# Weights on the ScalarE ring beside DMA transposes on the SyncE ring, with a new instruction order, in a mixer-and-MLP block

## The chip, the cores and the metric

The kernel runs on one core of one Trainium2 chip. The metric is device time in microseconds (us), the median of several executions. A profile's span is some 1 to 2.5 us shorter than the time of a whole execution, so spans are compared with spans and times with times. The granted TensorE clock is given as a share of full speed.

The engines: TensorE (PE in the profile, PEld its weight loads), VectorE (DVE), ScalarE (ACT), GpSimd (POOL) and SyncE (SP). SyncE and ScalarE can both issue DMA transfers. Each has its own DMA queue, called its ring here. In the DMA view q1 is the SyncE ring and q10 the ScalarE ring. A transfer's time "to landing" runs from its issue to the signal that it is complete. PSUM is the memory that TensorE's results go to and from which other engines copy them.

## The reference, cut to what matters

```python
B, S, D, F = 1, 2048, 512, 1792            # all bf16
h  = gelu(layernorm(x) @ w1)               # first layer
hs = shift(h, by channel quarter: +1, -1, +2, -2 tokens) @ w2
x1 = x + hs                                # the "mixing" product
return x1 + gelu(layernorm(x1) @ w3) @ w4  # second layer, "up" and "down"
```

Both normalized inputs have to be transposed (tokens to columns) before their product. There are 16 tiles of 128 tokens in each layer, so 32 transposes of 128x512.

## The kernel before

The program is a list of operations with their reads and writes. A small scheduling model, inside the kernel file, orders DVE, ScalarE, GpSimd and SyncE. TensorE's order is given by a script, and the loads' order by another. In the script `up1:g` and `up2:g` are the first and second layer's products over a group of tiles (the tables `GROUPS`), `mix:t` a mixing product and `down:t` a last product. `ty:n` turns tile n on TensorE (n from 16 up is the second layer), `sa` and `sb` turn the halves of tile 0. `warm` is products of zeros, `ra` and `rb` are the halves of tile 0's first-layer product, and `th:0` turns its result; every tile that the script does not name is turned by a DMA transpose on SyncE.

```python
GROUPS = {1: (1, 1, 1, 1, 2, 1, 4, 2, 2, 1), 2: (2, 4, 4, 2, 4)}
LOADS = """
x1 x2 tp2 x0@act w1a w1b x3 x4-5 tp5 w2a w2b x6-7 w3 tp17 w4a x8-10 w4b tp6 x11-12 tp1 tp16 x13-15
"""
SCRIPT = """
warm:9 sa:0 sb:0 ty:1 ra:0 rb:0 ty:2 up1:1 th:0 up1:2 mix:0 ty:3 ty:5 mix:1 ty:4 up1:3-4 ty:16 mix:2 ty:17
mix:3 up2:0 mix:4 up1:5 down:1 down:0 ...
"""
...
            if q not in pe_tp:                      # not named in the script
                pg.add("sp", f"tp{q}",
                       lambda e: e.dma_start(xT[:, :, P * t : P * (t + 1)], xn_buf[:, slot(q), :], transpose=True), ...)
```

So the loads all leave on SyncE except x0 (`@act`), in one ring, and each engine runs its own list strictly in order. The eight tiles that TensorE needs first (0 to 5, and the second layer's 0 and 1) are turned on TensorE itself.

## Time and profile before

| | before |
|---|---|
| time, median (first session) | 135.79 us |
| span | 134.6 us |
| TensorE busy | 130.9 us (97%) |
| DMA transposes / tiles turned on TensorE | 24 / 8 |
| issue to landing of a DMA transpose, median | 2.5 us |
| waits of TensorE | 0.7 us for w1, 0.4 us for the zeros of the warm-up |

The lines that carry this stand in the prediction below. The table says that TensorE is the bound, that it hardly ever waits, and that its first real product waits for w1.

### The profile page before, as it was taken

The numbers are of one execution on the slowest core, as the hardware profiler recorded it, in microseconds if no ns is written. First come the engines' busy times: TensorE is split into PE (matmuls) and PEld (weight loads), VectorE is DVE, ScalarE is ACT, GpSimd is POOL, SyncE is SP. The second block draws the span as 40 slices with busy tenths as digits, with TensorE's granted clock in tenths as the row PEclk, the third lists the DMA queues.
The fourth block names the chain that finished last, engine by engine and source line by source line (L and its number), as shares of the span: only waits on it lengthen the run. The fifth ranks groups of instructions, "written<-read, shape, count | busy, mean of one in ns | idle before, by whom it ended". The sixth has DMA issues, their size and how long they took to land.

```text
span 134.6 us, 2001 instructions
## 1 busy us (share of the span) xinstructions
PE 130.9 (97%) x776; PEld 71.5 (53%) x789; DVE 50.8 (38%) x134; ACT 58.4 (43%) x92; POOL 29.7 (22%) x68
## 2 busy tenths in 40 slices
PE   8799999999999999999999999999999999999994
PEld 3287688544656444478544444444444444444464
DVE  2689996856178930070061004232222200012222
ACT  5779349989544275547315554000000155520000
POOL 2444549892102860006010001200000000000000
DMA  5999998445452134100411000211111100001112
GB/s 136 323 345 399 361 304 234 90 81 105 90 115 85 24 75 98 39 0 0 83 39 39 0 0 0 65 52 44 39 39 53 64 0 0 0 5 39 39 39 78
DMA packets 21289, 12.19 MB, mean 91 GB/s; under 512 B 13856, under 2 KB 20768, under 8 KB 21280
## 3 DMA queue, kind: packets, MB, share of 16 engines
q1 hardware_dynamic: 20704, 11.80, 32.7%
q10 hardware_dynamic: 576, 0.26, 0.7%
q8 instruction: 6, 0.10, 0.3%
q14 instruction: 3, 0.02, 0.1%
HBM read 6.82 MB, written 2.10 MB: 66 GB/s over the span
## 4 chain that ended last, share of the span: by engine, by line
PE 93%; DMA 4%; SPq 1%; issue 1%; DVE 0%
PE y_ps L626 46%; PE o_ps L695 36%; PE o_ps L666 10%; DMA w_sb<-in_w_dram 4%; PE y_ps L490 1%; SPq L368 1%; PE y_ps L528 0%; SPq L377 0%; DVE o_sb L703 0%; PE o_ps L594 0%; SPq L857 0%
## 5 line engine op out<-in xcount | busy, mean ns | idle before, releaser
L626 PE MATMUL y_ps<-xnT,w_sb 128*128 128x512 bf16 (+2 forms) x421 | 63.4, 308 | 0.2
L626 PEld LDWEIGHTS y_ps<-xnT,w_sb 128*128 128x128 bf16 x424 | 38.3, 98 | 24.8
L641 ACT ACTIVATE h2T<-y_ps 128x1024 bf16<-128x1024 f32 (+1 forms) x29 | 28.6, 993 | 48.8 <-PE y_ps L626 48.6
L695 PE MATMUL o_ps<-w_sb,h2T 128*128 128x512 bf16 (+3 forms) x247 | 48.6, 355 | 0.3
L695 PEld LDWEIGHTS o_ps<-w_sb,h2T 128*128 128x128 bf16 x252 | 23.5, 98 | 24.7
L703 DVE TENSOR_TENSOR o_sb<-o_ps,x_sb 128x512 bf16<-128x512 f32 (+3 forms) x18 | 11.4, 632 | 47.1 <-PE o_ps L695 47.1
L423 POOL TENSOR_TENSOR rstd<-mv,neghalf 128x1 f32<-128x1 f32 x21 | 11.5, 549 | 23.6 <-DVE mv L418 14.8
L416 DVE BATCH_NORM_STATS2 st<-x_sb 128x6 f32<-128x512 bf16 x21 | 14.1, 678 | 3.4 <-DMA x_sb<-in_x_dram 3.2
L666 PE MATMUL o_ps<-w_sb,hT 128*128 128x512 bf16 x59 | 14.9, 379 | 0.3
L423 POOL TENSOR_TENSOR rstd<-vpe,neghalf 128x1 f32<-128x1 f32 x11 | 6.0, 547 | 29.4 <-DVE vpe L412 29.3
L673 DVE SCALAR_TENSOR_TENSOR x_sb<-o_ps,x_sb 128x512 bf16<-128x512 f32 x5 | 3.4, 686 | 19.2 <-PE o_ps L666 19.2
L641 ACT ACTIVATE hT<-y_ps 128x512 bf16<-128x512 f32 (+1 forms) x10 | 8.1, 807 | 5.5 <-PE y_ps L626 5.3
L677 DVE TENSOR_TENSOR x_sb<-o_ps,x_sb 128x512 bf16<-128x512 f32 x11 | 7.6, 687 | 4.4 <-PE o_ps L666 4.1
L666 PEld LDWEIGHTS o_ps<-w_sb,hT 128*128 128x128 bf16 x64 | 6.0, 98 | 5.7
L457 POOL TENSOR_SCALAR xn_buf<-x_sb,rstd,nmr 128x512 bf16<-128x512 bf16 x11 | 8.4, 765 | 0.8 <-DVE nmr L450 0.4
L400 ACT ACTIVATE junk<-x_sb 128x512 bf16<-128x512 bf16 x11 | 6.9, 624 | 2.2 <-DVE x_sb L673 2.2
L454 ACT ACTIVATE xn_buf<-x_sb,nmr,rstd 128x512 bf16<-128x512 bf16 x8 | 6.3, 806 | 0.6 <-POOL nmr L450 0.6
L445 DVE TENSOR_SCALAR xn_buf<-x_sb,mv,rstd 128x512 bf16<-128x512 bf16 x12 | 5.3, 442 | 2.8 <-POOL rstd L423 2.6
L720 PE MATMUL o_ps<-zeros 128*128 128x512 bf16 x9 | 4.0, 631 | 0.4 <-DVE zeros L347 0.4
L395 ACT ACTIVATE junk<-x_sb 128x512 bf16<-128x512 bf16 x6 | 3.7, 624 | 0.8 <-DMA x_sb<-in_x_dram 0.8
L418 DVE BATCH_NORM_AGGREGATE mv<-st 128x2 f32<-128x9 f32 x21 | 3.8, 189 | 0.3
L450 POOL TENSOR_SCALAR nmr<-mv,rstd 128x1 f32<-128x1 f32 x13 | 3.4, 263 | 0.7
(34 smaller groups left out, 28.6 us busy)
## 6 DMA issues: line engine op xcount, KB each, us to landing
out_dram<-o_sb SPq DMA_DIRECT2D x15, 128.0 KB, 1.7
w_sb<-in_w_dram SPq DMA_DIRECT2D x1, 1792.0 KB, 9.7
w_sb<-in_w_dram SPq DMA_DIRECT2D x2, 896.0 KB, 11.5
w_sb<-in_w_dram SPq DMA_DIRECT2D x4, 256.0 KB, 5.2
x_sb<-in_x_dram SPq DMA_DIRECT2D x3, 256.0 KB, 5.1
x_sb<-in_x_dram SPq DMA_DIRECT2D x2, 384.0 KB, 8.9
x_sb<-in_x_dram SPq DMA_DIRECT2D x3, 128.0 KB, 2.6
xnT<-xn_buf SPq DMA_TRANSPOSE x24, 2.5
```

What stands on the lines that cost most here:

```text
L400: (lambda d: (lambda e: e.activation(d, src, ACT_F.Square, accum_out=sums[:, q, 1:2])))(junk[:, b, :]),
L416: pg.add("dve", f"bnst{q}", lambda e: e.bn_stats(st9[:, q, 0:6], src), reads=rs, writes=[(("st", q), 0)], dur=605)
L423: lambda e: e.tensor_tensor(col(rstd), var, neghalf[:], ALU.pow),
L445: lambda e: e.tensor_scalar(dst, src, mv[:, q, 0:1], rstd[:, q : q + 1], ALU.subtract, ALU.mult),
L454: f = lambda e: e.activation(dst, src, ACT_F.Identity, bias=nmr[:, q : q + 1], scale=rstd[:, q : q + 1])
L457: f = lambda e: e.tensor_scalar(dst, src, rstd[:, q : q + 1], nmr[:, q : q + 1], ALU.mult, ALU.add)
L626: ins = e.matmul(y_ps[:, p, W * i : W * (i + 1)], wsb[:, dc, P * fc : P * (fc + 1)], src[:, dc, P * t0 : P * t0 + W], start=(dc == 0), sto ...
L641: (lambda d, s: (lambda e: e.activation(d, s, ACT_F.Gelu_apprx_tanh)))(dst, ysrc),
L666: ins = e.matmul(dst, hT[:, j, c0 : c0 + P], w2_sb[:, j, :], start=(j == 0), stop=(j == DC - 1))
L677: f = lambda e: e.tensor_tensor(x1_sb[:, t, :], dst, x_sb[:, t, :], ALU.add)
L695: ins = e.matmul(dst, h2T[:, fc, P * t : P * (t + 1)], w4_sb[:, fc, cs], start=(fc == 0), stop=(fc == FC - 1))
L703: (lambda d, c: (lambda e: e.tensor_tensor(o_sb[:, oi, c], d, x1_sb[:, t, c], ALU.add)))(dst, cs),
```

## The change

The intent is to free TensorE from three transposes and to keep the remaining DMA transposes out of the queue of the big weight loads. w3 and w4, and three pairs of x tiles, leave on ScalarE's ring. Each is held back until a named ScalarE instruction has been issued (`>ev1act`). The order of everything was searched anew with the scheduling model. The core of the diff, other tables and the script's tail cut:

```diff
+        for a, b in self.gates:
+            assert named[a].eng == named[b].eng, (a, b)
+            order_only.add((named[a].idx, named[b].idx))
 ...
-                at = max(clock + 500.0, op.start + 2450.0, last + 600.0) + self.LAG["tp"]
+                at = max(clock + 500.0, op.start + 2450.0, last[op.eng] + 600.0) + self.LAG["tp"]
 ...
-GROUPS = {1: (1, 1, 1, 1, 2, 1, 4, 2, 2, 1), 2: (2, 4, 4, 2, 4)}
+GROUPS = {1: (1, 1, 1, 1, 1, 1, 1, 2, 2, 1, 4), 2: (1, 1, 4, 2, 4, 4)}
 LOADS = """
-x1 x2 tp2 x0@act w1a w1b x3 x4-5 tp5 w2a w2b x6-7 w3 tp17 w4a x8-10 w4b tp6 x11-12 tp1 tp16 x13-15
+x1-2 w3@act>ev1act x0 tp1 x9-10@act>gelu1_3_0 x14-15@act>norm0_1 x3 x12-13@act>norm0_1 w1a tp3 w1b x5 x4 x6
+w4@act>gelu1_4_0 x11 tp4 tp2 w2a w2b x7-8 tp26
 SCRIPT = """
-warm:9 sa:0 sb:0 ty:1 ra:0 rb:0 ty:2 up1:1 th:0 up1:2 mix:0 ty:3 ty:5 mix:1 ty:4 up1:3-4 ty:16 mix:2 ty:17
-mix:3 up2:0 ...
+warm:13 sa:0 ty:2 sb:0 ty:1 ra:0 rb:0 up1:2 ty:3 th:0 up1:1 up1:3 mix:1 ty:4 mix:0 up1:4 mix:2 up1:5 mix:3
+up1:6 mix:4 up1:9 mix:5 up2:1 up1:7 up2:0 ...
```

The changed line with `last[op.eng]` is a belief about the hardware in the model: a transpose waits for earlier loads of its own ring only.

More of the change, by code (lines that the diff above doesn't have):

```diff
@@ L31 @@
     LOOK = {"dve": 300.0, "act": 300.0}
-    DUE = 164483.0
+    DUE = 2578.37
     BEGIN = {"sp": 30.0, "act": 150.0, "pe": 400.0, "dve": 150.0, "pool": 450.0}
@@ L40, in __init__ @@
         self.lines = []
+        self.gates = []
     def add(self, eng, name, fn, reads=(), writes=(), dur=100.0, queue=None):
@@ L161, in place @@
         fed = {}
-        clock = moved = last = self.total = 0.0
+        clock = moved = self.total = 0.0
+        last = {"sp": 0.0, "act": 0.0}
         out = []
@@ L198, in land @@
         def land(op):
-            nonlocal moved, last
+            nonlocal moved
             if op.queue == "tp":
-                at = max(clock + 500.0, op.start + 2450.0, last + 600.0) + self.LAG["tp"]
+                at = max(clock + 500.0, op.start + 2450.0, last[op.eng] + 600.0) + self.LAG["tp"]
             elif op.name.startswith("out"):
@@ L209, in land @@
             if op.queue != "tp":
-                last = max(last, at)
+                last[op.eng] = max(last[op.eng], at)
             op.landed = at
@@ L258, in place @@
         return out
-GROUPS = {1: (1, 1, 1, 1, 2, 1, 4, 2, 2, 1), 2: (2, 4, 4, 2, 4)}
-NORM = {0: "act", 3: "act", 7: "pool", 8: "act", 9: "pool", 10: "pool", 11: "pool", 12: "pool", 14: "act", 15: "act", 16: "pool", 18: "act", 19: "act", 24: "pool", 25: "act", 26: "pool", 27: "pool", 29: "pool", 30: "pool", 31: "act"}
-EVAC = {0: "both", 1: "both", 2: "both", 4: "both", 8: "both", 9: "dve", 10: "dve", 11: "dve", 12: "dve", 13: "dve", 14: "dve", 16: "dve", 17: "dve", 19: "both", 20: "both", 21: "both", 22: "both", 23: "both", 24: "dve", 25: "both", 27: "both", 29: "both", 30: "both", 31: "both"}
-STAT_ACT = (0, 7, 9, 12, 13, 15, 18, 21, 25, 29, 30)
+GROUPS = {1: (1, 1, 1, 1, 1, 1, 1, 2, 2, 1, 4), 2: (1, 1, 4, 2, 4, 4)}
+NORM = {0: "act", 4: "act", 8: "act", 10: "act", 11: "pool", 13: "act", 14: "act", 15: "pool", 16: "act", 18: "pool", 19: "pool", 20: "pool", 21: "act", 22: "act", 24: "pool", 25: "pool", 30: "act", 31: "pool"}
+EVAC = {0: "dve", 1: "both", 3: "both", 4: "dve", 5: "both", 6: "both", 7: "both", 8: "dve", 9: "dve", 11: "dve", 12: "both", 13: "dve", 15: "dve", 16: "both", 17: "both", 18: "dve", 19: "both", 20: "both", 23: "dve", 24: "both", 25: "both", 27: "dve", 30: "both", 31: "dve"}
+STAT_ACT = (0, 15, 16, 17, 18, 21, 24, 25, 29, 30)
 TAIL = (256, 160, 96)
-NMR = {0: "pool", 1: "pool", 3: "pool", 5: "pool", 6: "pool", 7: "pool", 8: "pool", 9: "pool", 11: "pool", 13: "pool", 14: "pool", 15: "pool", 16: "pool", 17: "pool", 18: "pool", 20: "pool", 21: "pool", 22: "pool", 26: "pool", 27: "pool", 28: "pool", 29: "pool", 31: "pool"}
+NMR = {0: "pool", 1: "pool", 4: "pool", 5: "pool", 6: "pool", 7: "pool", 8: "pool", 9: "pool", 10: "pool", 11: "pool", 13: "pool", 14: "pool", 15: "pool", 17: "pool", 19: "pool", 20: "pool", 21: "pool", 24: "pool", 29: "pool", 30: "pool"}
 NAT = (0,)
@@ L268 @@
 CSPLIT = ()
-HEV = {0: "dve", 4: "dve"}
-BIAS = {}
+HEV = {1: "dve", 3: "dve", 6: "dve"}
+BIAS = {"bnag0": 683.678, "bnag11": -581.289, "bnag3": -802.143, "bnag4": -247.442, "bnst1": 1925.74, "bnst10": -711, "bnst18": -352, "bnst7": -21, "mean11": -569, "mean15": -1694, "nmr17": -616, "nmr6": -709, "norm17": 1723.03, "norm3": 232.064, "ssq21": 621.832, "sum9": 1546, "tp13": -978.761, "tp15": 365.734, "tp21": -782, "x1_10": -3, "x1_9": -111}
 LOADS = """
-x1 x2 tp2 x0@act w1a w1b x3 x4-5 tp5 w2a w2b x6-7 w3 tp17 w4a x8-10 w4b tp6 x11-12 tp1 tp16 x13-15
+x1-2 w3@act>ev1act x0 tp1 x9-10@act>gelu1_3_0 x14-15@act>norm0_1 x3 x12-13@act>norm0_1 w1a tp3 w1b x5 x4 x6
+w4@act>gelu1_4_0 x11 tp4 tp2 w2a w2b x7-8 tp26
 """
 SCRIPT = """
-warm:9 sa:0 sb:0 ty:1 ra:0 rb:0 ty:2 up1:1 th:0 up1:2 mix:0 ty:3 ty:5 mix:1 ty:4 up1:3-4 ty:16 mix:2 ty:17
-mix:3 up2:0 mix:4 up1:5 down:1 down:0 mix:5 up1:6-7 mix:8 mix:6 up1:9 mix:9-10 up1:8 mix:7 mix:11 up2:1
-mix:13 mix:15 up2:3 down:5 mix:12 up2:2 mix:14 down:2 down:4 down:3 down:6-8 down:11 down:9 up2:4 down:10
-down:12-15
+warm:13 sa:0 ty:2 sb:0 ty:1 ra:0 rb:0 up1:2 ty:3 th:0 up1:1 up1:3 mix:1 ty:4 mix:0 up1:4 mix:2 up1:5 mix:3
+up1:6 mix:4 up1:9 mix:5 up2:1 up1:7 up2:0 mix:7 mix:6 up1:8 down:0 mix:8 up1:10 mix:10 mix:9 up2:2 mix:14
+down:1 mix:11 up2:3 mix:13 down:2-3 down:6 mix:15 up2:4 mix:12 down:7 down:4-5 down:8-9 up2:5 down:10
+down:12 down:11 down:14 down:13 down:15
 """
@@ L363, in load @@
             name, _, eng = item.partition("@")
-            eng = eng or "sp"
+            eng = eng.partition(">")[0] or "sp"
             if name[0] == "x":
@@ L744, in bass_standalone__mixer_s_mlp__prompt_kernel @@
                     op.first = i - 100
+                    if ">" in item:
+                        pg.gates.append((item.partition(">")[2], op.name))
                     queues[op.eng].append(op.name)
```

## The prediction

> **What bounds the kernel now.** I read the page's busy line first, then the chain that ended last, then the waits and the start in order of time.
>
> ```profile
> PE 130.9 (97%) x776; PEld 71.5 (53%) x789; DVE 50.8 (38%) x134; ACT 58.4 (43%) x92; POOL 29.7 (22%) x68
> PE 93%; DMA 4%; SPq 1%; issue 1%; DVE 0%
> ```
>
> The reader is to see that TensorE is busy for 130.9 of 134.6 us, and that 93% of the chain that sets the end is TensorE itself. The other engines have room over the whole span. The opening part of the chain, in order of time, and two stretches from its middle:
>
> ```profile
> 0.99 0.43 SPq L377
> 1.47 5.13 DMA w_sb<-in_w_dram
> 6.65 0.61 PE y_ps L528 x2
> ...
> 8.60 0.92 PE y_ps L626 x16
> ...
> 12.02 2.64 PE y_ps L626 x32
> ...
> 24.70 6.04 PE o_ps L695 x28
> ```
>
> One wait stands at the head: the second half of w1, issued at about 1.47 us, releases the second half of the first tile's row product (L528) at 6.65 us. After it the chain has only TensorE entries, and no "issue" entry over 0.05 us. The last product ends at 132.87 us, where the chain passes to the last DVE add. So after 6.65 us there are 126.2 us with hardly a gap. The waits of TensorE confirm this; there are only two:
>
> ```profile
> PE y_ps L528 <- DMA w_sb<-in_w_dram: 0.7, 1, 0.7
> PE o_ps L720 <- DVE zeros L347: 0.4, 1, 0.4
> ```
>
> Only two things can move the time much: the TensorE work that stands after w1, and the moment at which w1 lands. New stalls are the third, and they can only add. The busy table by stretch (TensorE, weight load, DVE, ScalarE, GpSimd, clock, DMA share, GB/s) shows where a stall would come easily:
>
> ```profile
> 7.00:17.00 10.00, 9.90 (x112) 7.61 (x112) 9.37 (x26) 6.94 (x14) 4.54 (x9) 1.00 1.05 368
> 17.00:31.00 14.00, 13.95 (x104) 9.41 (x103) 10.23 (x36) 11.54 (x26) 11.40 (x23) 1.00 0.81 172
> 60.00:90.00 30.00, 29.84 (x158) 15.59 (x160) 5.98 (x16) 12.14 (x14) 4.15 (x8) 1.00 0.13 31
> ```
>
> From 7 to 17 us DVE is 94% busy and the DMA engines are full at 368 GB/s. After 60 us nothing but TensorE is loaded. The change acts in the tight part.
>
> **What the Trainium skill says.** "TensorE: Matmul & The Clock Gate", section "Wait — 56ns, not 53.3ns?", gives a warm matmul as its columns over 2.4 GHz plus about 2.5 ns. The trace agrees: 28 products of 512 columns take 6.04 us (216 ns each), and 16 of 128 columns take 0.92 us at most (57 ns each; 16 x 55.8 = 0.89 us). I count work by it. "DMA: Bandwidth & Descriptors", section "Issuing engines are not separate DMA queues", says that transfers issued from ScalarE and SyncE share the same 16 DMA engines, so a second ring saves issue time only. Its section "Queues, rings and completion order" adds that each DMA engine takes turns between rings packet by packet. Before, the ScalarE ring carries a single tile and the last store, so its trace can't show how two loaded rings share. One side of it shows: in one common ring, the first transpose, issued at 15.96 us amid the weight loads, took 5.9 us to land, and the median one 2.5 us.
>
> ```profile
> DMA to landing us min/median/max: 2.4/2.5/5.9
> ```
>
> **The change part by part.**
>
> TensorE transposes. Before, eight tiles are turned on TensorE (tile 0 in halves, 1, 2, 3, 4, 5 and the second-layer tiles 0 and 1). Two of them stand ahead of the first w1 product, in time that is waiting anyway. Six lie on the path. At four 128-column passes of 55.8 ns each that is 6 x 0.223 = 1.34 us. After, five are turned on TensorE (0, 1, 2, 3, 4); 0, 2 and 1 are now before the w1 product, so two lie on the path: 0.45 us. Saved: 0.89 us. The other three go to DMA transposes on the SyncE ring (24 become 27).
>
> Groups. The first layer's products over groups of one tile cost 16 x 55.8 = 0.893 us, of two tiles 16 x 109.2 = 1.747 us, of four 16 x 215.8 = 3.453 us. Before, beside tile 0: five single, three double, one quadruple, 13.16 us. After: seven single, two double, one quadruple, 13.20 us. Cost: 0.04 us. The second layer has 56 products a group: 3.125, 6.115 and 12.085 us. Before (2,4,4,2,4): 48.49 us. After (1,1,4,2,4,4): 48.62 us. Cost: 0.13 us. The mixing products and the down products are the same, and so is the tail of the last tile.
>
> Sum of work on the path: -0.89 + 0.17 = -0.72 us.
>
> The head. Before, SyncE issues x1, x2, w1a, w1b, with x0 on ScalarE. After, SyncE issues x1-2 (one transfer), x0, x3, w1a, w1b. w1b is the fifth issue and no longer the fourth, at some 0.45 us each (0.87 us for the first two), and one more tile of 131 KB lies ahead of it, which at the 330 to 350 GB/s of this stretch is 0.38 us. These two overlap, so I don't add them: w1b lands about 0.4 us later, near 7.0 us. The 13 warming products (9 before, 9 took 4.02 us) and four transposes, by an estimate from the rows of the start, are through at 6 to 6.7 us: still under w1. So the start costs +0.4 us.
>
> The loads. w3 leaves on ScalarE after tile 1's evacuation (some 6.5 us, from a like step at 5.6 to 6.0 us before), x9-10 and the rest after a GELU near 11 us, w4 after another near 14.5 us. Adding the new order's durations from 7.0 us, the second-layer product that first needs w3 comes at 20 us and the first down product at 31 us. Before, w3 took 9.7 us from issue to landing in full queues; from 6.5 us that is 16 us, in time. w4 (11.5 us a half before) lands by about 26 us, in time. Their going earlier or later is worth nothing in itself: both were hidden.
>
> The ordering elsewhere (which engine normalizes or evacuates a tile, the biases) moves work between engines that are not the bound. No gain to count where TensorE has no gaps.
>
> Sum: -0.72 + 0.4 = -0.3 us if nothing stalls. That would be 135.5 us.
>
> **The rivals.**
>
> First, w2 becomes a wait. Before, 1.83 MB go through the ring up to w2b and the first mixing product starts at 9.57 us, its weights loading at 9.30. After, four single tiles and x11 lie ahead of w2b, 2.10 MB; the extra 0.26 MB at 345 GB/s is 0.76 us, so about 10.1 us, while the new order needs it at about 10.6 us (7.0 + 0.45 + three single groups at 0.89 + two transposes at 0.22 + half a product's start). That is a margin of half a microsecond, and w3's packets come in from about 8 us. They are 3,584 bytes a row against w2's 1,024, so if rings take turns by packet w3 gets the larger share. If so the mixing product waits 0.5 to 3 us, and that early in a dense kernel the wait goes straight to the end. Against it: w3's issue is gated, by 8 us most of w2's bytes have gone out.
>
> Second, the transposes beside w3. The new order's first product with a DMA-transposed tile is the single group 5, at about 14.7 us, where before the first such product came at about 22 us. The tile is loaded and normalized by perhaps 10.5 us (some 2.5 us of statistics, power, scale with DVE full). At 2.5 us it lands at 13 us, in time; at the 5.9 us seen amid loads it lands past 16 us and TensorE stands for 1.5 to 2 us. What speaks for the first is the purpose of the change: the transposes are no longer behind the weights in one ring.
>
> Third, ScalarE blocked by issuing. On SyncE the issues behind a full ring took 3.59 us (x8-10) and 1.83 us (w4b), where an ordinary one takes 0.45. The same on ScalarE, for w4 near 14.5 us with x tiles queued ahead, would hold up the GELUs that the mixing products need. SyncE has nothing else to do; ScalarE has, at 69% to 82% busy in the tight stretches. Cost: 0 to 2 us.
>
> Fourth, the start: with the hole in the DMA rate at 2.7 to 3.3 us before (41 to 184 GB/s) the added tile could be free, which gives back up to 0.4 us.
>
> **Range and chances.** The floor is the path without new stalls and with a free head: 135.79 - 0.72 - 0.35 (all remaining gaps closed) = 134.7 us. A gain of over 2% needs 133.1 us, 1.6 us below that, so it is next to excluded. Without stalls it is 135.1 to 135.5; small stalls of 0.2 us or so are likely, and one of the first three rivals in full gives 136.5 to 138. I put a third on one of them costing more than 0.5 us, and a twelfth on them summing to the 2.7 us that make it slower by 2%. I take 135.5 us, with a range of 134.7 to 137.2.
>
> **What would show it.** TensorE transposes (L490) at 20 instructions in place of 32; the first-layer row product's release at about 7.0 us by w1; TensorE's own waits still only w1 and the zeros. If a wait of the mixing product for w2 appears near 11 us, the first rival is right; if one of an up product for a DMA-transposed tile appears at 15 to 18 us, the second; if ScalarE shows issues of 1 us or more and TensorE waits for GELU results, the third. If w1 is released at 6.6 us the fourth holds. The prediction is wrong if the new waits sum to over 2 us, or if the gain is over 1.1 us, which would mean that gaps I counted as 0.35 us in the dense part were larger.

## The result, and the profile after

The changed kernel took 143.3 us (143.04 to 143.81, four runs) against 135.78 us in the same session. The ratio is 1.0554, 95% interval 1.0491 to 1.0617. Ratios here and below are the mean time of one kernel's fast runs over that of the other's of the same rounds, so not quite the ratio of the medians quoted. All four runs: their spans were 140.8 to 142.5 us and their mean clocks 0.976 to 0.988.

The page of the changed kernel: busy time by engine, then three rows of the 40 slices (3.5 us each), then the chain that ended last:

```profile
PE 133.8 (95%) x853; PEld 73.8 (52%) x853; DVE 51.2 (36%) x139; ACT 56.0 (40%) x82; POOL 27.5 (19%) x64
...
PE   8899079999999999999999999999999999999994
...
PEclk9999856999999999999999999999999999999999
DMA  4999999991565421003102112001211100011112
...
PE 86%; DMA 9%; DVE 1%; POOL 1%; SPq 1%; issue 0%; DVEq 0%
```

TensorE has a hole in the fifth slice (14 to 17.6 us). From that slice on the granted clock is down for three slices. The DMA row stays at 9 through the hole. The share of the chain that is DMA has risen from 4% to 9%. The chain in order of time (start, length, what):

```profile
3.06 4.32 DMA x_sb<-in_x_dram
...
9.94 0.41 DVE xn_buf L452
10.35 0.03 DVE mv L425
10.38 8.15 DMA xnT<-xn_buf
18.53 0.05 issue
18.58 1.89 PE y_ps L633 x16
20.47 1.71 PE o_ps L673 x4
```

Tile 5 is scaled by 10.35 us and its transpose is issued at 10.38. It lands at 18.53, after 8.15 us where the median was 2.5 before. Its product follows at once, and 16 matmuls take 1.89 us where 16 took 0.89 us at full clock. TensorE's own list of waits has one large entry:

```profile
PE y_ps L633 <- DMA xnT<-xn_buf: 4.4, 1, 4.4
```

The stretches of the hole (TensorE, weight load, DVE, ScalarE, GpSimd, clock, DMA share, GB/s):

```profile
15.00:16.00 1.00, 0.00 (x0) 0.00 (x0) 0.94 (x3) 0.00 (x0) 0.77 (x2) 1.00 0.81 134
16.00:17.00 1.00, 0.00 (x0) 0.00 (x0) 0.00 (x0) 0.00 (x0) 0.12 (x1) 0.87 1.09 267
17.00:18.00 1.00, 0.00 (x0) 0.00 (x0) 0.00 (x0) 0.00 (x0) 0.00 (x0) 0.50 1.79 198
18.00:19.00 1.00, 0.42 (x5) 0.43 (x6) 0.00 (x0) 0.00 (x0) 0.00 (x0) 0.50 0.83 159
...
23.00:24.00 1.00, 1.00 (x11) 0.83 (x9) 0.73 (x5) 0.17 (x1) 0.91 (x2) 0.71 0.99 316
```

Between 16.2 and 18.5 us no compute engine does anything at all: every one of them stands at a place of its list that needs, directly or through another engine, what this one transpose releases. The DMA engines are busy but move 134 to 267 GB/s, where in the stretch from 7 to 17 us the kernel before moved 368. The clock falls at 16.75 us and is back at 23.6.

The span's account closes. The work on TensorE's path is 0.72 us less, as counted in the prediction. The hole costs 4.41 us. From 18.58 to 23.6 us TensorE works 5.0 us at half clock, which loses 2.5 us. Together that is +6.2 us, and the spans differ by 140.8 - 134.6 = 6.2 us. Whether the 2.5 us could be had back by itself is another question, which the first experiment asks.

### The profile page after: what moved, and what is told of

Same layout as the page of the kernel before. It is cut to its first block, busy times and chain, and to the rows that moved or that the text cites. A ratio compares the mean times of both kernels' runs of the same rounds, so it can differ in the third digit from the quotient of the medians.

```text
span 140.8 us, 2139 instructions
## 1 busy us (share of the span) xinstructions
PE 133.8 (95%) x853; PEld 73.8 (52%) x853; DVE 51.2 (36%) x139; ACT 56.0 (40%) x82; POOL 27.5 (19%) x64
## 3 DMA queue, kind: packets, MB, share of 16 engines
q10 hardware_dynamic: 3584, 4.59, 11.5%
## 4 chain that ended last, share of the span: by engine, by line
PE 86%; DMA 9%; DVE 1%; POOL 1%; SPq 1%; issue 0%; DVEq 0%
PE y_ps L633 43%; PE o_ps L702 34%; PE o_ps L673 9%; DMA xnT<-xn_buf 6%; DMA x_sb<-in_x_dram 3%; POOL rstd L430 1%; DVE st L423 1%; SPq L375 0%; DVE xn_buf L452 0%; SPq L384 0%; POOL nmr L457 0%; DVE o_sb L710 0%; DVE mv L425 0%; DVEq L830 0%
## 5 line engine op out<-in xcount | busy, mean ns | idle before, releaser
L633 PE MATMUL y_ps<-xnT,w_sb 128*128 128x128 bf16 (+2 forms) x496 | 65.6, 294 | 4.4 <-DMA xnT<-xn_buf 4.4
L633 PEld LDWEIGHTS y_ps<-xnT,w_sb 128*128 128x128 bf16 x496 | 41.1, 101 | 29.6 <-DMA xnT<-xn_buf 4.9
L648 ACT ACTIVATE h2T<-y_ps 128x1024 bf16<-128x1024 f32 (+2 forms) x29 | 28.7, 994 | 43.5 <-PE y_ps L633 43.3
L702 PEld LDWEIGHTS o_ps<-w_sb,h2T 128*128 128x128 bf16 x252 | 23.6, 98 | 24.9
L673 PE MATMUL o_ps<-w_sb,hT 128*128 128x512 bf16 x64 | 17.0, 395 | 0.0
L423 DVE BATCH_NORM_STATS2 st<-x_sb 128x6 f32<-128x512 bf16 x22 | 14.7, 674 | 2.8 <-DMA x_sb<-in_x_dram 2.7
L684 DVE TENSOR_TENSOR x_sb<-o_ps,x_sb 128x512 bf16<-128x512 f32 x8 | 5.5, 686 | 21.6 <-PE o_ps L673 21.5
L680 DVE SCALAR_TENSOR_TENSOR x_sb<-o_ps,x_sb 128x512 bf16<-128x512 f32 x8 | 5.4, 686 | 13.6 <-PE o_ps L673 13.6
L407 ACT ACTIVATE junk<-x_sb 128x512 bf16<-128x512 bf16 x10 | 6.2, 624 | 6.6 <-DVE x_sb L680 6.6
L452 DVE TENSOR_SCALAR xn_buf<-x_sb,mv,rstd 128x512 bf16<-128x512 bf16 x14 | 6.5, 465 | 3.8 <-POOL rstd L430 3.8
L464 POOL TENSOR_SCALAR xn_buf<-x_sb,rstd,nmr 128x512 bf16<-128x512 bf16 x8 | 6.1, 770 | 1.1 <-DVE nmr L457 0.9
L727 PEld LDWEIGHTS o_ps<-zeros 128*128 128x128 bf16 x13 | 1.5, 123 | 2.7 <-issue 1.7
```

Of the source, the lines that this page charges most:

```text
L407: (lambda d: (lambda e: e.activation(d, src, ACT_F.Square, accum_out=sums[:, q, 1:2])))(junk[:, b, :]),
L423: pg.add("dve", f"bnst{q}", lambda e: e.bn_stats(st9[:, q, 0:6], src), reads=rs, writes=[(("st", q), 0)], dur=605)
L452: lambda e: e.tensor_scalar(dst, src, mv[:, q, 0:1], rstd[:, q : q + 1], ALU.subtract, ALU.mult),
L464: f = lambda e: e.tensor_scalar(dst, src, rstd[:, q : q + 1], nmr[:, q : q + 1], ALU.mult, ALU.add)
L633: ins = e.matmul(y_ps[:, p, W * i : W * (i + 1)], wsb[:, dc, P * fc : P * (fc + 1)], src[:, dc, P * t0 : P * t0 + W], start=(dc == 0), sto ...
L648: (lambda d, s: (lambda e: e.activation(d, s, ACT_F.Gelu_apprx_tanh)))(dst, ysrc),
```

## The experiments

Three theories stand for the 8.2 us. **A:** a ring is served transfer by transfer, so the transpose waited for all of w3. **B:** the rings take turns packet by packet, so each small packet of a transpose waits for a row of the loads. **C:** what was issued earlier goes first, whatever its ring. A second question is whether the lateness of these few transposes is the whole loss. Line numbers differ between the kernels by a few lines, since the edits add some.

**1. The hole filled.** 18 products of zeros were put ahead of tile 5's product; the order of everything else is unchanged.

```diff
+    pg.add("pe", "fill", fill, reads=[(("zeros",), 0)], writes=pair_rv(p, v - 0.5), dur=0.0)   # 18 x 128x512
     pg.add("pe", f"up{layer}_{g}_{f0}", f, ...      # only for layer 1, group 5
```

> The changed kernel with 18 products of zeros (3.9 us at full clock) put ahead of the first-layer product of tile 5, where TensorE stood still for 4.4 us; nothing else moves. Theory: 4.4 us of the loss is the wait for the DMA transpose of tile 5, and 2.5 us more is the half clock from 16.75 to 23.6 us that the idle time brought (5.0 us of work at half speed). Then the transpose still lands near 18.5 us, the clock stays at 1.00, and the time is about 143.3 - 2.5 = 140.8 us. Rival: the clock fell for another reason, or the stretch after it waits for other transposes anyway; then the time stays at 143 us.

Measured: 142.17 us, ratio 1.0515 (1.0463 to 1.0567), clock 1.00, span 141.9 us. TensorE in order of time:

```profile
14.22 4.05 PE L642 MATMUL y_ps<-zeros 128*128 128x512 bf16 x18
18.95 1.07 PE L633 MATMUL y_ps<-xnT,w_sb 128*128 128x128 bf16 x16 [0.68 <-DMA xnT<-xn_buf]
19.85 1.03 PE L682 MATMUL o_ps<-w_sb,hT 128*128 128x512 bf16 x4
22.28 1.07 PE L633 MATMUL y_ps<-xnT,w_sb 128*128 128x128 bf16 x16 [1.40 <-DMA xnT<-xn_buf]
```

The clock held, so the idle time had brought it down. But the 2.5 us did not come back in full: the two ratios differ by only 0.5 us' worth, and their intervals overlap. (The execution profiled, 143.33 us, is the longest of the four; the others took 141.96 to 142.31.) TensorE at full clock waits for the next transpose, tile 6, until 22.28 us. The changed kernel's own trace says how much could come back. Its first four transposes landed at 18.53, 20.72, 23.13 and 25.29 us, and the product with the last of them began at 26.41. At full clock it could have begun just after 25.29, so some 1 us of the 2.5 was there to be had (an estimate from these landings). The rest was hidden behind the next transposes, which set the pace, one after another.

**2. w3 in four transfers,** as four row blocks (rows of 3,584 bytes as before) and as four column blocks (rows of 896 bytes); everything else is unchanged.

```diff
-   e.dma_start(w3_sb[:], whole)
+   [e.dma_start(dst[:, c : c + 1, :], whole[:, c : c + 1, :]) for c in range(4)]                                    # row blocks
+   [e.dma_start(dst[:, :, cols * k : cols * (k + 1)], whole[:, :, cols * k : cols * (k + 1)]) for k in range(4)]   # column blocks
```

> The changed kernel with w3 issued as four transfers of 448 KB (one after another at the same place on the ScalarE ring, same 3,584-byte rows, same order of everything else). Theory A, a ring is served transfer by transfer: the transpose of tile 5 goes in between two pieces, its landing falls from 8.2 us to 4 to 5 us, and TensorE's wait from 4.4 to about 1 us, 139 to 140 us. Theory B, the sharing goes by packets and the size of w3's rows is what counts: no change, 8 us and 143 us. Theory C, everything issued earlier goes first whatever its ring: no change either.

> The changed kernel with w3 issued as four column blocks: 448 KB each again, but rows of 896 bytes in place of 3,584. Theory A, transfer by transfer: as with the four row blocks, 4 to 5 us for the transpose of tile 5. Theory B, packet by packet: here too it gets its turns, four times as often, so its landing falls to 4 to 5 us while the row blocks leave it at 8 us. Theory C, order of issue whatever the ring: still 8 us in both.

Measured: 144.01 us (ratio 1.0634, 1.0562 to 1.0705) and 145.06 us (1.0711, 1.0638 to 1.0784). Tile 5's transpose took 8.4 and 8.6 us to land. Theory A falls. Theory B in the form "the size of w3's rows counts" falls as well. The packet records of the trace show why neither edit could help: in the changed kernel the transpose's first packet was moved at 14.25 us, 3.9 us after its issue, just as the last of w3's 512 rows had started (14.24). After that its packets went beside the x tiles that follow on the same ring more than beside w3.

**3. Tiles 5, 6, 11 and 17 back on TensorE,** first right ahead of their use, then one mixing product earlier.

```diff
-up1:5 mix:3 up1:6 mix:4 up1:9 mix:5 up2:1
+ty:5 up1:5 mix:3 ty:6 up1:6 mix:4 ty:11 up1:9 mix:5 ty:17 up2:1                  # e2_pe_tp
-mix:2 up1:5 mix:3 up1:6 mix:4 up1:9 mix:5 up2:1
+ty:5 mix:2 up1:5 ty:6 mix:3 up1:6 ty:11 mix:4 up1:9 ty:17 mix:5 up2:1            # e6_pe_ahead
```

> The changed kernel with tiles 5, 6 and 11 of the first layer and tile 1 of the second turned on TensorE again (4 x 0.22 = 0.9 us more work). Theory: the DMA transposes of these early tiles are the whole loss; the stall of 4.4 us and the half clock (2.5 us) both go, so 143.3 - 6.9 + 0.9 = 137.3 us, down to 136.5 if the time before outside the span shrinks too. Rival: the next DMA-transposed tiles (7, 8, then tile 0 of the second layer) are as late, so that a stall of 1 us or more comes up near 22 to 26 us and the time stays above 139 us.

> The changed kernel with tiles 5, 6, 11 and second-layer tile 1 turned on TensorE, this time one mixing product ahead of their use, so that the evacuation is hidden (with the turn just ahead of its use TensorE waited 0.8 to 0.9 us for the copy four times, 140.7 us). Theory: the loss is the lateness of these four DMA transposes and nothing else; what remains over before is 0.17 us of work: 135.5 to 137 us. Rival: more comes up later (transposes of tiles 7, 8 and second-layer tile 0 while w4 flows): above 138 us.

Measured: 140.71 us (ratio 1.041, 1.0357 to 1.0464) and 139.28 us (1.0279, 1.025 to 1.0309). In the first form TensorE waits 0.8 to 0.9 us four times, because the copy out of PSUM stands right between turn and use; that edit was clumsy. In the second form a single wait is left:

```profile
PE y_ps L633 <- DMA xnT<-xn_buf: 1.9, 1, 1.9
```

So turning these four tiles on TensorE takes away about half of the loss (1.0554 to 1.0279), although it adds some 0.9 us of work. The rival of the expectation was right about the rest. The next DMA transposes, of tiles 7 and 8, are late too: up to 6.9 us to land.

**4. w4 held back** in that second form, until just ahead of the first second-layer GELU.

> The version with tiles 5, 6, 11 and second-layer tile 1 turned on TensorE one product ahead (139.3 us), with w4 alone held back on ScalarE until just ahead of the first second-layer GELU (near 22 us in place of 13.5). Theory: the 1.9 us that TensorE still waited there for the transpose of tile 7 or 8 (6.9 us from issue to landing) is w4's doing; without it those transposes land in 3 us and the wait goes: 137.2 to 138 us, as long as w4 lands before the first down product (near 33 us). Rival: the x tiles on that ring are what delays them, and the wait stays at 1.5 us or more; or w4 becomes the wait, which gives 139 us or more.

Measured: 143.33 us (the three fast runs of four; 143.91 with the slow one), ratio 1.0623 (1.0586 to 1.066). The 137.2 to 138 us of the theory were missed. Its first half came true: the transposes of tiles 7 and 8 landed after 3.0 and 2.5 us, and the wait for them is gone; TensorE runs through from 20.89 to 25.9 us. Then it waits for the transpose of second-layer tile 0, which now lies beside w4:

```profile
PE y_ps L633 <- DMA xnT<-xn_buf: 4.0, 1, 4.0
```

The chain in order of time shows its length:

```profile
21.52 8.31 DMA xnT<-xn_buf
```

The 8.3 us follow the load to wherever it is put.

**5. ScalarE's loads held back** in the changed kernel: w3 and the x tiles until 13.3 us; then only the x tiles and w4.

```diff
+   held = [op for op in pg.seq if op.name in ('dma_w3', 'dma_x9', 'dma_x14', 'dma_x12')]   # to just ahead of dma_w4
+   held = [op for op in pg.seq if op.name in ('dma_x9', 'dma_x14', 'dma_x12', 'dma_w4')]   # to just ahead of gelu1_5_0
```

> The changed kernel with the order of all compute unchanged, but w3 and the three x transfers held on ScalarE until just ahead of w4 (near 13.4 us instead of 6.4 and 10.5 to 11.9 us). Theory: without loads on the other ring the transpose of tile 5 takes about 2.5 us from issue to landing (lands near 13 us), tile 6 lands near 14.2, and TensorE does not wait for either; instead the first product with w3 waits some 3 us near 19 to 22 us. Time 138 to 140.5 us. Rival: the transposes are slow in this stretch for a reason of their own (the busy SyncE ring[...]): landing stays at 6 us or more with the ScalarE ring silent.

> The changed kernel with w3 where it is (6.4 us), but the three x transfers and w4 held until ahead of the GELU of tile 5 (near 14.5 us). Theory: the delay has two parts, a start behind w3 and a slow passage beside the rows that follow it; w3 alone lets the transpose of tile 5 land right after w3's last rows, near 15 to 16 us in place of 18.5, so TensorE waits about 1 to 1.5 us. If only w3 counts, no change to 18.5 us; if only the x rows count, it lands near 13 us.

Measured, w3 held: 143.71 us, ratio 1.0606 (1.0556 to 1.0657). Tile 5's transpose landed after 4.3 us in place of 8.2, and TensorE waited 0.41 us for it. So most of the lateness goes with the other ring's traffic. The expected 2.5 us were not reached: 449 of its 512 packets were moved between 11 and 12 us, the others only by 13.65, and why is not shown. The second half of the expectation failed: w3's rows ran from 14.45 us on, tile 6's transpose landed only at 18.56, after 7.1 us, and TensorE waited 2.15 us for it:

```profile
14.52 1.07 PE L633 MATMUL y_ps<-xnT,w_sb 128*128 128x128 bf16 x16 [0.41 <-DMA xnT<-xn_buf]
...
18.61 1.07 PE L633 MATMUL y_ps<-xnT,w_sb 128*128 128x128 bf16 x16 [2.15 <-DMA xnT<-xn_buf]
```

The transposes that followed were late too, and the time did not move:

```profile
PE y_ps L633 <- DMA xnT<-xn_buf: 6.9, 4, 2.7
```

Measured, x tiles held: two runs of 140.19 and 142.6 us, and the profile counts as slow by that spread, so no time is drawn from them. The trace, of the longer run, gives 6.3 us to landing for tile 5's transpose and a wait of 2.43 us for it. Its landing lies between that of the changed kernel and that with w3 held. This suggests, from one slow run, that both parts of the traffic count, as expected, though the wait was larger than the 1 to 1.5 us I gave.

**6. The ring alone** in the order of the kernel before: w3 and w4 (in halves) on ScalarE, everything else there as it was.

```diff
-... w3 tp17 w4a x8-10 w4b tp6 ...
+... w3@act>ev1act tp17 w4a@act>gelu1_4_0 x8-10 w4b@act tp6 ...
```

> The ring alone: the tables, groups and TensorE order of the kernel before, with w3 on the ScalarE ring after tile 1's evacuation and w4 in two halves on it after the GELU of tiles 4-5; everything else stays on SyncE. Theory: the ring does harm only where a DMA transpose is needed while loads run on the other ring; here the first one is needed near 22 us, so the time stays within 1 us of before (134.8 to 136.8 us), and the first transpose still takes 5 us or more to land. Rival: loads on a second ring slow everything early (w2, the x tiles), and the time is 137 us or more.

Measured: 138.46 us (the three fast runs of four, 137.8 to 139.73; 139.09 with the slow one), ratio 1.0194 (1.0142 to 1.0247). It is slower, though whether by 2% is unclear. My expectation was wrong and its rival right: the second ring does harm even where no early product needs a DMA transpose. The first transpose, issued at 15.30 us, took 8.1 us to land. The x tiles 11 and 12, issued behind it on SyncE at 16.77, took 7.1 us. DVE, which runs its list in order, stood for them, and TensorE waited 2.0 us, until 32.6 us, for a PSUM bank that DVE had not emptied. In the execution profiled (139.73 us) the clock then fell to half for 3.4 us, which cost some 1.7 us more; the two shorter fast runs kept a mean clock of 1.00.

**7. The disputed cost by itself.** A kernel that only measures (its result is x, wrong): sixteen transposes on SyncE in four groups of four. ScalarE's ring is silent in groups 1 and 4, runs w3 twice in group 2 and w4 twice in group 3.

> Not the kernel but a measurement (its result is x, so it is wrong on purpose): sixteen DMA transposes of 128x512 on the SyncE ring in four groups of four. Group 1 with the ScalarE ring silent, group 2 while w3 runs twice on the ScalarE ring (rows of 3,584 bytes), group 3 while w4 runs twice on it (rows of 1,024 bytes), group 4 silent again. Theory, the rings take turns packet by packet: a transpose is 32 packets of 256 bytes on each of 16 DMA engines, 18 ns each; beside rows of 1,024 bytes (46 ns) 32 x 64 ns = 2.05 us a transpose, beside rows of 3,584 bytes (140 ns) 32 x 158 ns = 5.06 us. So the landings of one group follow one another by 1.3 us (issue-bound) in groups 1 and 4, by about 2 us in group 3 and about 5 us in group 2, and the first of a group lands after 2.5 us, 5 to 6 us and 8 us or more. Rival, the second ring only waits for what was issued before it: the first of a group is late in groups 2 and 3, but the later ones follow by 1.3 us.

Issue to landing, groups 1 to 4 in turn:

```profile
DMA to landing us min/median/max: 2.5/2.5/2.5
...
DMA to landing us min/median/max: 4.5/6.5/7.5
...
DMA to landing us min/median/max: 7.1/7.6/8.1
...
DMA to landing us min/median/max: 2.4/2.5/2.5
```

The same instruction on the same data takes 2.5 us beside a silent ring (group 1) and 7.1 to 8.1 us beside w4 (group 3); beside w3, which ends during group 2, it takes 4.5 to 7.5 us. This is the size of the 8.2 us of the changed kernel, with no other part of it present. It has two parts.

The first part is the passage. In group 3 the first two transposes, issued at 32.80 and 34.05 us, landed after 7.3 and 8.1 us, at 40.09 and 42.18: 2.09 us apart, where 2.05 was predicted from taking turns. The estimate behind it comes from packet records of the traces. A transpose is 512 packets of 256 bytes, 32 on each of 16 DMA engines, at 18 ns; a load's row of 1,024 bytes takes 46 ns; 32 x (18 + 46) ns = 2.05 us. The records show it directly. While both rings are full, as many packets of the one kind as of the other are moved. Here are a microsecond beside w3's rows of 3,584 bytes (24 to 25 us) and one beside w4's of 1,024 bytes (40 to 41 us); behind the queue stand packets, MB and share of time:

```profile
q10 hardware_dynamic: 108, 0.39, 95.8%
q1 hardware_dynamic: 108, 0.03, 13.7%
...
q10 hardware_dynamic: 281, 0.29, 81.0%
q1 hardware_dynamic: 275, 0.07, 30.9%
```

This is theory B.

The second part is the start. The first packet of a group moved 1.2 us after its issue with the other ring silent (9.59 against 8.35 us). Beside loads it moved 4.0 us (23.40 against 19.45) and 4.3 us (37.15 against 32.80) after. These 3 us hardly depend on the row size, 3,584 or 1,024 bytes. Something is served ahead of the newcomer, as theory C has it, but for a limited time. What it is stays open. Because of it, w3 was through by 26.1 us, before the first transpose of group 2 was; so no whole transpose passed beside w3. But the microsecond shown above was all overlap, and at its 108 packets a transpose of 512 would take 4.7 us (an estimate), near the 5 us expected.

In the changed kernel the two parts do not add up to the 8.15 us. By the packet records tile 5's start took 3.9 us and the first 512 transpose packets 2.5 us (to 16.7), and the landing came 1.8 us after that, where it came 0.5 us after in group 1. From 17.4 to 18.5 us some twenty packets of both rings took 0.6 to 1.1 us each. What held them is not shown.

**8. One ring with the new order.** First with the scheduling model run again, and with tile 5 on TensorE in addition; then with every engine's order kept as in the changed kernel and only the five loads moved.

```diff
+x1-2 x0 tp1 x3 w1a tp3 w1b x5 x4 x6 tp4 tp2 x11 w2a w2b x7-8 w3 tp5 tp6 tp11 tp17 x9-10 tp7 tp8 x14-15 x12-13 tp16 w4 tp26   # e12; e13 with ty:5 too
+before = {"dma_w3": "tp5", "dma_x9": "tp8", "dma_x14": "sum15", "dma_x12": "sum15", "dma_w4": "tp13"}   # e15: placed ahead of these, on SyncE
```

> The changed kernel's TensorE order with every load on the SyncE ring: w3 behind x7-8, then the transposes of tiles 5, 6, 11 and second-layer tile 1, x9-10, tiles 7 and 8, the x tiles 12 to 15, second-layer tile 0, w4, the rest. Theory, two rings taking turns are what makes transposes slow: behind w3 in the same ring the transpose of tile 5 starts when w3's last row is through (about 14.2 us) and lands near 15.3 us in place of 18.5, the next ones 1.3 us apart and not 2.2; TensorE waits about 1 us once, and the time is 136.5 to 138 us. Rival, it is the sum of the transfers that this order wants early: the same waits come back elsewhere (x tiles, w4), 141 us or more.

> The same single ring with tile 5 alone turned on TensorE, one mixing product ahead of its use (0.22 us more work). Theory: the wait of about 1 us behind w3 goes, and what is left is 0.72 - 0.22 = 0.5 us less work than before: 135.0 to 135.6 us, the first version of the new order that is level with the kernel before or just under it. Rival: the next transpose (tile 6) or the later x tiles become the wait: 136.5 us or more.

> The changed kernel with the order of all compute and of all transposes as it is; only the five loads that ScalarE issued go to the SyncE ring: w3 ahead of the transpose of tile 5, x9-10 after the transpose of second-layer tile 1, the other x tiles after that of tile 7, w4 after that of tile 9. Theory, turn-taking of two rings is the cause: tile 5 lands near 15.3 us (right behind w3) and not at 18.5, the next three 1 to 1.5 us apart; TensorE waits about 1 us for tile 5, perhaps 1 us more for x tiles or w4, and the clock holds: 136 to 138 us. Rival, the sum of the transfers is: waits of 4 us and more in other places, 140 us or more.

Measured: 142.09 us (ratio 1.0478, 1.0441 to 1.0515), 139.8 us (1.0331, 1.0306 to 1.0356) and 142.4 us (1.0481, 1.0429 to 1.0533). All three missed the theory's range and fell in the rival's. The first two lost 2.25 us to a late scaling of tile 4 on ScalarE, which the rerun model had moved, so their times say little about the ring. In the second TensorE waited only 0.6 us for DMA transposes; the same kernel with tile 4 scaled in time was not run. The third is the clean one; its TensorE waits:

```profile
PE y_ps L633 <- DMA xnT<-xn_buf: 3.9, 2, 2.6
PE o_ps L702 <- DVE st L423: 1.6, 1, 1.6
```

And SyncE's own list in order of time (start, length, line, operation, count):

```profile
16.60 0.58 SPq L375 DMA_DIRECT2D x_sb<-in_x_dram  x1
19.24 2.63 SPq L470 DMA_TRANSPOSE xnT<-xn_buf  x2
21.92 1.09 SPq L375 DMA_DIRECT2D x_sb<-in_x_dram  x2
```

Tile 5's transpose landed at 16.77 us in place of 18.53, TensorE's wait for it fell from 4.41 to 2.64 us, and by the packet records the next three passed in 0.5 to 0.6 us each. So one ring does cure the slow passage of these three. Tile 5 itself still took 6.6 us, behind w3 in the same ring (w3 landed at 16.28). But SyncE issues in order too. The last x tiles leave only at 21.92 and 22.54 us, behind transposes whose tiles were not ready. The very last land 5.2 us after their issue, DVE stands 3.4 us for them, and the loss is back.

**9. Small steps on the kernel before,** to see whether a part of the change is worth keeping.

```diff
-ty:1 ra:0 rb:0 ty:2      -x0@act w1a w1b
+ty:1 ty:2 ra:0 rb:0      +x0@act w1a@act w1b
```

> The kernel before, with one step taken from the changed kernel: tile 2 is turned on TensorE ahead of the first w1 product and not after it, in time in which TensorE waits for w1 anyway. Theory: 0.22 us of work leaves the path, 135.2 us against 135.4, a ratio of 0.998. Rival: the turn waits for tile 2's scaling and holds up the first product: 1.000 or above.

> The kernel before, with the first half of w1 issued on ScalarE behind x0, so that w1's second half is SyncE's third issue and not its fourth. Two rings share without transposes here. Theory: w1b leaves 0.45 us earlier and TensorE starts 0.2 to 0.4 us earlier, ratio 0.997 to 0.999. Rival: the x tiles that follow on SyncE now share with w1a, or ScalarE's table load and first statistics come later, and the start is the same or later: ratio 1.000 to 1.005.

Measured: 135.98 us, ratio 1.0061 (1.0043 to 1.0078), and 135.48 us, ratio 1.0019 (0.9994 to 1.0044), against 135.21 us. Neither helps. In the second, w1a landed early (3.5 us) and TensorE then waited 0.85 us for w1b, until 6.80 us, against 6.65 before: the start is no earlier. In the first, the spans (134.4 to 135.3 us) are as much longer than those of the kernel before in the same session (133.7 to 134.2) as the times are; what costs the 0.6% was not looked into. No version that was run beats the kernel before.

## Why the prediction was wrong

**The work was right.** TensorE turned five tiles in place of eight, and the span's account closes with the counted -0.72 us.

**The head was sized wrong, without consequence.** I put w1b 0.4 us later. The second half of the first row product started at about 6.68 us against 6.65, so the added tile was free. That was the fourth rival. The error moved the prediction 0.4 us up and so hid a little of the larger one.

**The first and third rivals did not come.** No mixing product waited for w2. ScalarE's issues of w3 and w4 took 0.44 and 0.40 us.

**The step that failed is the landing of the first DMA transposes: assumed in time in the sum, and too small in the second rival.** The sum of 135.5 us took tile 5's transpose as landing at 13 us, 2.5 us after its issue, with no wait. The second rival had the right place and the right cause ("the single group 5, at about 14.7 us"). But it took the 5.9 us of the one transpose seen amid loads, in one ring, as the worst case, and gave the wait as "1.5 to 2 us". Measured were 8.2 us and 4.4 us. I then weighed it down with "What speaks for the first is the purpose of the change: the transposes are no longer behind the weights in one ring." The intent of an edit is no evidence. The skill's sentence on turns packet by packet, which the prediction quoted for w2, applied to the transposes with more force: their packets are a quarter the size of w2's rows. The page before gives 13,856 packets under 512 bytes for 24 transposes, so some 36 on each of 16 engines, and 368 GB/s is a row of 1,024 bytes every 45 ns on each engine: a passage of about 2 us could have been worked out. The late start could not. The trace before has one like it (the first packet of that 5.9 us transpose moved 3.0 us after its issue), but there the loads stood ahead of it in the same ring. Experiment 7 measured both parts by themselves.

**I also counted one late transpose where there was a train of them.** Experiment 1 shows that after tile 5 the next is waited for, and experiments 4 and 5 that removing one wait brings up the next. The range's top, "one of the first three rivals in full gives 136.5 to 138", assumed one wait of 2 us. Behind the first late landing stood three more, each 2.2 to 2.4 us after the last, so that curing the first alone gives little back.

**The clock was not in the prediction.** It fell to half and cost 2.5 us on the books. By experiment 1 and the landings some 1.5 us of that was hidden behind the waits that followed. The 1 us left is an estimate and within the noise of the ratios, so the clock is at most a small part of the result.

What is shown: transposes on one ring take 4.5 to 8.1 us beside loads on the other and 2.5 us alone (experiment 7), the new order needs such transposes from 14.2 us on, and the loss moves with the loads when these are moved (experiments 4, 5 and 8). What is not shown: that no placement of the loads could make the new order pay. Several were tried, and in each a wait came up somewhere else, but of the 4.4 us that the one-ring version with tile 5 on TensorE lost, 2.25 went by one misplaced scaling that was not put right. What serves the loads ahead of a new transpose for some 3 us also stays open.

## What to carry to other kernels

A second ring is not a second set of DMA engines. Before a small-packet transfer with a deadline is put beside a bulk load, work out its passage as (its packets on each engine) x (its packet + the other ring's packet), add some 3 us for the start (the 2.7 to 3.1 us of experiment 7), and compare with the moment at which the bound engine needs it. When a kernel is bound by one engine without gaps, freeing 0.9 us of its work by handing it to a resource that is full at that moment buys a wait. And when one wait is removed and the time stays, look for the next arrival of the same kind before looking for another cause.

## What the Trainium skill lacked or had wrong

- "DMA: Bandwidth & Descriptors", sections "Issuing engines are not separate DMA queues" and "Queues, rings and completion order": the passage of 2.09 us a transpose beside 1,024-byte rows, and 108 packets of one ring beside 108 of the other in a microsecond of 3,584-byte rows, agree with turns packet by packet. (A packet of the trace is a single row; the page's packet holds several descriptors. Equal counts do not tell whether turns were taken row by row.) The page says that a second issuing engine saves only issue time, not that it can cost: w3 and w4 moved to the second ring, with TensorE's order as it was, gave +1.9% (138.46 us). It also lacks the late start: a transpose's first packet came 4.0 to 4.3 us after issue beside loads and 1.2 us after it alone.
- The same page, section "Latency and other measured facts", states 261 GB/s for the DMA transposes of one kernel, with a non-contiguous middle dimension. Here four transposes of 131 KB back to back, with nothing beside them, were issued every 1.31 us (1.26 us each on the issuing engine), which is 100 GB/s; issuing is the limit at this size.
- "TensorE: Matmul & The Clock Gate", section "What's actually happening", gives a free-running idle window of about 3.4 us. Idle times well under that can be enough: here the clock fell 2.6 us into the gap (at 16.75 us, from 14.17), and in experiment 6 it fell in the execution whose longest gap was 2.04 us. In experiment 8 a gap of 2.64 us left it at 1.00 in the third kernel, while the first, with 2.25 us as its longest wait, had a mean clock of 0.988.
